# One ScalarE operation for phi of 18 sums, small operations moved to GpSimd, and a new order of all instructions

## The chip, the cores and the metric

The program runs on one core of a Trainium2 chip. The metric is the device time of one execution in microseconds, the median of three runs. A core has five engines with an in-order queue each: TensorE (PE in the profile; its weight loads PEld), VectorE (DVE), ScalarE (ACT), GpSimd (POOL) and SyncE (SP), which here only issues DMAs. They wait for one another by semaphores.

## The reference, cut to what matters

```python
x  = A_x                                   # 2048 tokens x 512, fp32
xn = layernorm(x)
q, k, v = split(xn @ wqkv)                 # 32 heads of 16
phi = lambda t: where(t > 0, t + 1, exp(t)) + 1e-6
kv, z = einsum(phi(k), v), sum(phi(k))     # per head
s  = (phi(q) @ kv / (phi(q) . z + 1e-6)) @ wo
g  = silu((gelu(x @ w_gate) * (x @ w_up)) @ w_down)    # of the same xn; F = 1792
out = x + s * g
```

## The kernel before, in words

Everything is fp32 made from pairs: each operand is split into a high part `h` (rounded) and a low part `l` (the rest), and each product is three TensorE passes, h·h, h·l and l·h. On top of that the large products use a seven-product Strassen scheme (`PRODUCTS`), in three PSUM banks X, Y and Z: product 1 goes into X, ScalarE copies X to Y (the "seed"), product 2 is added to Y and product 6 to X; ScalarE saves X (`u2`), product 7 is added, X is saved again (`u3`), product 4 is added to X, and products 5 and 3 go into Z. VectorE adds a saved tile and Z (`added`, tiles `c22` and `c12`).

The 2048 tokens are 16 tiles of 128, taken as 8 pairs `n`. Per pair, for q and k:

- `ln` normalises: statistics on VectorE (`bn_stats`, `bn_aggr`), the addition of eps to the variance (`ve`, VectorE), a power of -1/2 on GpSimd (`rstd`), and xn on VectorE (first pairs) or ScalarE (`xn`, with bias and scale from tiles).
- xn is turned: the first pairs by TensorE (`pt`), the later ones by a write to DRAM (`xn_d`), a read (`xq`) and VectorE's transpose (`xt`).
- `forms` makes the Strassen sums `T` on GpSimd; `split` makes `Xh` (ScalarE) and `Xl` (VectorE).
- Pairs 0 and 1 take plain products, pairs 2 to 7 the scheme above. Of each pair there are four results: k from Y, q from c22, q from X, k from c12. `phi` turns each into phi by two ScalarE operations, relu(-v) into a tile `r` and exp(-r) in place (L708, L709), and one VectorE operation max(v,0)+r into a tile `p0` (L711; `kp` or `qp` in the trace). `r` has two places and `p0` four, taken in turn, so a new `qp` waits until the DMA of the one four before it (`q_d<-qp`) has landed.
- `split_xn` sets a column of xn to one (L686, VectorE) and splits xn; `gacc` then accumulates xn^T·phi(k) in four PSUM banks (`gps`); the column of ones gives the sum z.

Meanwhile some FFN weights are prepared (`tmp`, `we`, written to `w_d`). From about 125 us on the FFN runs in two halves of 1024 tokens with gate, up and down products (FX, FY, FZ and dX, dY, dZ), and the attention's last product (`sps`) is put between its last passes.

The order of the instructions on every engine is set by one list of numbers, `ORDER`: the code records some 3600 operations with their dependencies, and `plan.order()` emits them as the list says. The list was searched beforehand with a model of durations and of transfer times that were scattered at random.

Of the kernel before, what the change touches and what calls it, by code (L numbers as in the profile page):

```python
# [18 lines left out]
    2, 4, 1, 0, 993, 3, 6, 7, 9, 10, 11, 8, 16, 15, 17, 23, 5, 18, 19, 14, 55, 24, 13, 12, 56, 27, 57, 20, 58, 115, 61, 60, 62, 28, 64, 116, 117, 66,  # L19
    68, 118, 59, 25, 119, 67, 89, 88, 35, 120, 65, 80, 26, 91, 82, 74, 93, 79, 121, 21, 77, 104, 122, 90, 123, 124, 22, 33, 148, 98, 149, 36, 126, 73,  # L20
    71, 69, 38, 76, 72, 151, 102, 95, 34, 63, 132, 78, 75, 96, 37, 108, 81, 150, 105, 94, 313, 140, 127, 83, 134, 141, 315, 99, 31, 287, 138, 100,
    125, 136, 314, 289, 131, 84, 101, 133, 288, 152, 316, 142, 153, 290, 103, 92, 139, 291, 137, 85, 319, 292, 135, 106, 317, 128, 107, 320, 109, 178,
    86, 170, 318, 173, 110, 181, 180, 293, 322, 425, 143, 158, 171, 167, 154, 295, 155, 111, 296, 70, 427, 174, 298, 172, 112, 176, 177, 129, 175,
    299, 426, 163, 297, 161, 230, 294, 29, 232, 428, 234, 401, 226, 300, 113, 233, 301, 321, 30, 179, 302, 229, 87, 164, 231, 144, 399, 307, 160, 224,
    182, 223, 145, 187, 305, 47, 165, 166, 32, 190, 183, 306, 225, 228, 400, 431, 156, 402, 245, 97, 239, 162, 309, 308, 243, 159, 184, 146, 244, 250,
    403, 227, 303, 39, 240, 404, 49, 241, 256, 328, 304, 311, 248, 40, 157, 258, 235, 323, 265, 263, 41, 266, 236, 255, 246, 114, 51, 264, 260, 42,
    262, 261, 208, 237, 257, 45, 259, 247, 405, 188, 249, 43, 429, 276, 407, 282, 267, 242, 46, 238, 281, 202, 185, 197, 196, 251, 279, 44, 273, 278,
    252, 272, 147, 919, 274, 277, 268, 253, 271, 275, 189, 269, 280, 254, 192, 283, 191, 186, 408, 284, 203, 310, 327, 168, 285, 325, 326, 52, 286,
    206, 331, 218, 199, 215, 410, 312, 193, 920, 341, 409, 411, 340, 324, 53, 342, 270, 130, 922, 332, 343, 367, 406, 333, 346, 921, 348, 169, 412,
    349, 923, 347, 511, 413, 350, 200, 54, 334, 415, 414, 198, 207, 335, 219, 417, 513, 194, 222, 336, 358, 512, 419, 514, 440, 210, 329, 337, 356,  # L30
    418, 924, 357, 479, 515, 211, 925, 926, 516, 359, 212, 201, 214, 614, 360, 927, 221, 195, 205, 420, 338, 361, 216, 209, 344, 517, 330, 362, 518,
    384, 438, 616, 439, 520, 519, 615, 217, 48, 437, 928, 521, 430, 204, 443, 386, 522, 213, 50, 220, 421, 930, 375, 444, 368, 422, 446, 423, 929,
    445, 523, 441, 617, 339, 345, 931, 447, 452, 618, 351, 619, 454, 528, 543, 453, 369, 940, 352, 385, 527, 455, 442, 381, 363, 353, 620, 376, 424,
    383, 623, 459, 354, 460, 932, 624, 529, 461, 365, 462, 364, 524, 448, 534, 380, 470, 621, 469, 449, 532, 525, 468, 622, 366, 379, 533, 934, 471,
    377, 416, 378, 355, 382, 526, 472, 456, 535, 631, 458, 450, 473, 457, 370, 933, 489, 540, 371, 463, 542, 935, 536, 541, 582, 625, 451, 477, 626,
    546, 432, 495, 474, 491, 538, 476, 372, 433, 556, 434, 539, 373, 494, 630, 555, 537, 936, 493, 435, 547, 464, 937, 557, 646, 549, 717, 941, 558,
    387, 632, 548, 530, 943, 393, 550, 562, 942, 374, 475, 465, 564, 944, 563, 627, 392, 565, 388, 637, 497, 490, 719, 480, 498, 635, 488, 551, 718,
    492, 720, 571, 466, 628, 636, 395, 573, 478, 572, 721, 552, 394, 722, 560, 481, 574, 487, 638, 391, 496, 818, 575, 561, 482, 397, 723, 576, 389,
    398, 724, 559, 531, 643, 629, 633, 725, 483, 644, 819, 566, 938, 645, 939, 820, 396, 649, 390, 580, 544, 821, 578, 822, 823, 639, 651, 545, 553,
    579, 659, 484, 726, 592, 650, 640, 567, 599, 727, 658, 581, 641, 467, 660, 634, 485, 728, 652, 824, 747, 642, 577, 661, 663, 583, 664, 554, 501,  # L40
    945, 486, 667, 568, 665, 732, 584, 509, 653, 947, 666, 946, 825, 507, 503, 569, 948, 500, 654, 601, 729, 436, 595, 591, 668, 502, 662, 655, 597,
    730, 674, 733, 590, 676, 675, 669, 736, 499, 677, 594, 786, 504, 600, 949, 737, 505, 678, 681, 950, 951, 738, 596, 740, 679, 510, 952, 506, 585,
    508, 685, 826, 593, 731, 739, 647, 744, 961, 745, 586, 746, 656, 587, 682, 750, 683, 648, 953, 702, 741, 759, 734, 955, 753, 588, 954, 751, 827,
    589, 752, 956, 742, 761, 657, 828, 693, 754, 570, 735, 608, 696, 684, 829, 760, 613, 743, 762, 701, 610, 606, 957, 607, 697, 609, 755, 958, 959,
    695, 603, 670, 604, 833, 756, 766, 962, 686, 960, 768, 680, 671, 602, 963, 612, 1200, 765, 672, 964, 699, 767, 830, 688, 764, 769, 611, 965, 763,
    834, 831, 605, 775, 966, 776, 832, 748, 837, 968, 777, 770, 700, 778, 704, 967, 698, 838, 598, 779, 703, 969, 783, 757, 780, 694, 999, 839, 782,
    841, 673, 784, 840, 835, 846, 689, 785, 845, 758, 803, 847, 970, 690, 864, 972, 851, 795, 971, 865, 771, 687, 973, 794, 691, 860, 842, 1094, 787,
    853, 692, 852, 772, 749, 861, 843, 862, 788, 974, 714, 854, 844, 863, 976, 805, 855, 866, 975, 715, 856, 773, 705, 977, 868, 848, 869, 836, 789,
    774, 857, 711, 781, 867, 790, 887, 1050, 716, 870, 800, 791, 710, 713, 1099, 801, 871, 877, 978, 1100, 708, 792, 796, 980, 876, 979, 872, 878,
    793, 981, 884, 1095, 873, 712, 997, 879, 706, 874, 707, 883, 1101, 1096, 808, 1102, 814, 875, 709, 885, 1097, 849, 807, 1138, 886, 817, 880, 812,  # L50
    798, 1201, 858, 804, 797, 799, 1098, 890, 859, 802, 806, 809, 891, 815, 1269, 811, 1105, 881, 904, 901, 1002, 895, 888, 892, 902, 896, 1108, 850,
# [107 lines left out]
    3569, 3560, 3545, 3566, 3568, 3529, 3470, 3617, 3471, 3562, 3561, 3469, 3474, 3475, 3585, 3538, 3463, 3464, 3465, 3575, 3466, 3570, 3573, 3591,  # L159
    3574, 3546, 3616, 3472, 3547, 3578, 3539, 3607, 3530, 3477, 3579, 3479, 3478, 3473, 3610, 3480, 3622, 3580, 3614, 3467, 3584, 3602, 3563, 3615,  # L160
    3586, 3564, 3608, 3571, 3476, 3623, 3606, 3587, 3609, 3619, 3601, 3588, 3600, 3628, 3611, 3572, 3627, 3620, 3599, 3612, 3621, 3624, 3531, 3625,
    3613, 3630, 3626, 3631, 3598, 3633, 3632, 3634, 3603, 3635, 3604, 3605,
]

TABLES = {"exp": "exp", "gelu": "gelu", "silu": "silu"}
# [1283 lines left out]
```

## Time and profile before

| what | value |
|---|---|
| runs | 568.57, 568.45, 567.86 us; median 568.45 |
| the profiled execution's own time | 568.69 us |
| its span, first to last instruction | 567.0 us |
| granted TensorE clock | 1.000 |
| PE busy | 556.9 us (98%), 2620 matmuls |
| DVE, ACT, POOL busy | 491.4 (87%), 358.1 (63%), 216.4 us (38%) |

A PE that is busy 98% of the span may still run slower than it could, since a matmul's end in the profile is modelled: a matmul that reads 512 columns is shown with 379 ns, while matmuls follow one another more closely than that. The distance from one start to the next is what tells of a wait. In the rows of the timeline the columns are: start in us, duration in us, engine, line, operation, written tile <- read tiles, shapes, count, and in brackets the idle time of the engine before it and what ended it. `SPq` is SyncE's queue issuing a DMA. A row with x2 or more is several instructions in a row, from the first start to the last end.

### The profile page before, as it was taken

How to read it: one execution, taken by the hardware profiler on the slowest of the kernel's cores; microseconds unless marked ns; L12 is line 12 of the kernel's file. 1: busy time of each engine (PE TensorE's matmuls, PEld its weight loads, DVE VectorE, ACT ScalarE, POOL GpSimd, SP SyncE). 2: the span in 40 equal slices, each digit the busy share in tenths (PEclk: the TensorE clock that was granted, in tenths of full speed). 3: DMA queues.
4: the chain of work that ended last, by engine and by line, in shares of the span. 5: the costliest groups of instructions: out<-in, count | busy, mean ns of one | idle time of the engine just before them, and what ended most of it. 6: DMA issues, size and time to landing. Idle time of an engine off the chain costs nothing.

```text
span 567.0 us, 7903 instructions
## 1 busy us (share of the span) xinstructions
PE 556.9 (98%) x2620; PEld 485.2 (86%) x2620; DVE 491.4 (87%) x793; ACT 358.1 (63%) x662; POOL 216.4 (38%) x222
## 2 busy tenths in 40 slices
PE   7999999999999999999999999999999999999996
PEld 6888887888988888888888888888888888888885
DVE  6999998797599999999978886956688898998996
ACT  5987888796667775663546267957553635465531
POOL 4724342436767867304045652410214040324000
PEclk9999999999999999999999999999999999999999
DMA  8577989887778865458867898886645567668885
GB/s 282 149 209 238 291 266 269 255 253 232 305 268 322 312 236 202 144 206 286 304 212 287 324 410 319 265 344 221 242 149 205 205 215 281 228 189 267 279 260 210
DMA packets 82362, 143.71 MB, mean 253 GB/s; under 512 B 5393, under 2 KB 50449, under 8 KB 78354
## 3 DMA queue, kind: packets, MB, share of 16 engines
q1 hardware_dynamic: 82322, 143.22, 74.0%
q8 instruction: 20, 0.33, 0.2%
q14 instruction: 20, 0.16, 0.1%
HBM read 89.19 MB, written 54.00 MB: 253 GB/s over the span
## 4 chain that ended last, share of the span: by engine, by line
PE 95%; DMA 2%; DVE 2%; ACT 1%; SPq 0%; issue 0%; DVEq 0%; ACTq 0%
PE FX L443 26%; PE dX L443 13%; PE FZ L443 13%; PE sps L443 7%; PE dY L443 6%; PE gps L443 6%; PE FY L443 6%; PE X L443 5%; PE dZ L443 3%; PE Z L443 3%; PE k L443 2%; PE q L443 2%; PE Y L443 1%; DMA x<-in_A_x 1%; DMA q_d<-qp 1%; PE pkv L978 1%
## 5 line engine op out<-in xcount | busy, mean ns | idle before, releaser
L443 PE MATMUL FX<-Xh,w 128*128 128x512 f32 x448 | 125.7, 379 | 0.0
L443 PEld LDWEIGHTS FX<-Xh,w 128*128 128x128 f32 x448 | 84.5, 189 | 12.0
L405 POOL TENSOR_TENSOR sums<-draw 128x256 f32<-128x256 f32 x28 | 24.6, 882 | 128.3 <-DMA draw<-in_B_w_down 77.3
L399 ACT COPY dY<-dX 128x512 f32<-128x512 f32 x56 | 32.1, 574 | 63.1 <-DVE acc L1109 39.4
L443 PE MATMUL FX<-Xl,w 128*128 128x512 f32 x224 | 66.3, 380 | 0.1
L443 PE MATMUL FZ<-Xh,w 128*128 128x512 f32 x224 | 64.3, 379 | 0.0
L1155 POOL TENSOR_TENSOR h<-h,g 128x512 f32<-128x512 f32 x28 | 39.8, 1422 | 50.6 <-DVE h L405 42.7
L399 ACT COPY fu<-FX 128x512 f32<-128x512 f32 x56 | 32.6, 584 | 33.6 <-PE FX L443 25.4
L405 POOL TENSOR_TENSOR tmp<-raw 128x256 f32<-128x256 f32 x28 | 26.7, 964 | 57.8 <-DVE we L405 22.7
L443 PEld LDWEIGHTS FX<-Xl,w 128*128 128x128 f32 x224 | 42.2, 189 | 6.3 <-PE dX L443 0.4
L443 PEld LDWEIGHTS FZ<-Xh,w 128*128 128x128 f32 x224 | 42.3, 189 | 6.0
L405 DVE TENSOR_TENSOR hfl<-sums,hfh 128x512 fp32r<-128x512 f32 x56 | 44.8, 804 | 2.2 <-ACT hfh L399 2.1
L443 PE MATMUL dX<-hfl,dh 128*128 128x512 f32 x112 | 41.7, 380 | 0.2 <-DVE hfl L405 0.2
L443 PE MATMUL dX<-hfh,dl 128*128 128x512 f32 x112 | 41.8, 380 | 0.0
L443 PE MATMUL dX<-hfh,dh 128*128 128x512 f32 x112 | 41.5, 379 | 0.0
L399 ACT CAST hfh<-sums 128x512 fp32r<-128x512 f32 x56 | 34.3, 620 | 10.2 <-DVE sums L405 8.9
L1109 DVE TENSOR_TENSOR acc<-acc,dY 128x512 f32<-128x512 f32 x48 | 32.6, 680 | 9.2 <-PE dY L443 9.2
L1109 DVE TENSOR_TENSOR acc<-acc,dX 128x512 f32<-128x512 f32 x48 | 32.5, 680 | 6.2 <-PE dX L443 5.8
L405 DVE TENSOR_TENSOR hfl<-h,hfh 128x512 fp32r<-128x512 f32 x42 | 32.6, 781 | 2.1 <-ACT hfh L399 2.0
L443 PE MATMUL FZ<-Xl,w 128*128 128x512 f32 x112 | 33.0, 379 | 0.0
L443 PE MATMUL FY<-Xh,w 128*128 128x512 f32 x112 | 33.0, 379 | 0.0
L946 POOL TENSOR_TENSOR qz<-qz,zq 128x512 f32<-128x512 f32 x16 | 23.1, 1442 | 21.5 <-DMA qz<-q_d 11.9
(217 smaller groups left out, 1473.4 us busy)
## 6 DMA issues: line engine op xcount, KB each, us to landing
w<-w_d SPq DMA_DIRECT2D x17, 1792.0 KB, 7.6
w_d<-w SPq DMA_DIRECT2D x11, 1792.0 KB, 8.4
draw<-in_B_w_down SPq DMA_DIRECT2D x14, 512.0 KB, 4.4
w_d<-we SPq DMA_DIRECT2D x18, 256.0 KB, 2.2
x<-in_A_x SPq DMA_DIRECT2D x16, 256.0 KB, 4.3
q_d<-qp SPq DMA_DIRECT2D x16, 256.0 KB, 3.3
qz<-q_d SPq DMA_DIRECT2D x16, 256.0 KB, 3.2
q<-q_d SPq DMA_DIRECT2D x16, 256.0 KB, 3.8
```

The lines of the kernel that those rows point to most:

```text
L399: do("ACT", act(n, src.psum), lambda o, i: nc.scalar.copy(o, i), dst, src, name=name)
L405: do(eng, c, lambda o, p, q: getattr(e, f"tensor_{op}")(o, p, q), dst, a, b, name=name)
L443: nc.tensor.matmul(o if r is None else o[:, r], a, turned(b), start=first, stop=made == self.passes[r], skip_group_check=self.on or r is n ...
L946: do("POOL", pool(D), lambda o, z: nc.gpsimd.tensor_mul(o, o, z.unsqueeze(1).to_broadcast([P, KT, P])), rows_of(q), zq, name="u")
L978: nc.tensor.matmul(o[:, g, :], ab[c][:, g * P:(g + 1) * P], ab[KT + c][:, g * P:(g + 1) * P], start=(c == 0), stop=(c == KT - 1))
L1109: do("DVE", dve(D), lambda o, i: nc.vector.tensor_add(o, o, i), o, ps, name="acc")
L1155: do("POOL", pool(NC), lambda o, i: nc.gpsimd.tensor_mul(o, o, i), h, g, name="h")
```

## The change

For v that is a sum of two tiles (c22, c12) the addition adds 1 as well, so that the tile holds v+1; for k from Y the seed copies X+1 into Y. phi is then max(v+1, min(exp(v),1)): one ScalarE operation exp with a bias tile of -1, and one VectorE operation. These are three of four results of pairs 2 to 7, 18 in all; the fourth (q from X) and the plain ones stay as they were. The eps addition to the variance and the column of ones go from VectorE to GpSimd. `XA` is an empty list, so its branches do nothing.

```diff
+    neg_one = tile_in("sm", "no", [P, 1], F32, "neg_one")
+    do("DVE", 0.1, lambda o: nc.vector.memset(o, -1.0), neg_one, port=False)
...
-        do("DVE", 0.1, lambda o, i: nc.vector.tensor_scalar_add(o, i, EPS_LN), ve, mv[:, :, 1])
+        do("POOL", 0.1, lambda o, i: nc.gpsimd.tensor_scalar_add(o, i, EPS_LN), ve, mv[:, :, 1])
...
-        do("DVE", 0.1, lambda o: nc.vector.memset(o, 1.0), (x[0] if isinstance(x, tuple) else x)[:, 0:1], name="one", port=False)
+        do("POOL", 0.12, lambda o: nc.gpsimd.memset(o, 1.0), (x[0] if isinstance(x, tuple) else x)[:, 0:1], name="one")
...
     def added(e, ps, name, places=("c", range(19, 22))):
         c = U(*places, name)
-        tt("DVE", "add", c, e, ps, D, name)
+        do("DVE", 0.6, lambda o, i, j: nc.vector.scalar_tensor_tensor(o, i, 1.0, j, op0=ALU.add, op1=ALU.add), c, ps, e, name=name)
...
-    def phi(v, t, nm):
+    def phi(v, t, nm, plus=False):
         r = U("r", range(22, 24), f"{nm}r{t}")
+        if plus or not v.psum:
+            do("ACT", act(D), lambda o, i, b: nc.scalar.activation(o, i, AF.Exp, bias=b), r, v, neg_one, name="exp")
+            p0 = U("p", range(24, 28), f"{nm}p{t}")
+            do("DVE", 0.6, lambda o, i, j: nc.vector.scalar_tensor_tensor(o, i, 1.0, j, op0=ALU.min, op1=ALU.max),
+               p0, r, v, name="phi")
+            return p0
         do("ACT", act(D), lambda o, i: nc.scalar.activation(o, i, AF.Relu, scale=-1.0), r, v, name="relu")
         do("ACT", act(D), lambda o, i: nc.scalar.activation(o, o, AF.Exp, scale=-1.0), r, r, name="exp")
...
-        copy("ACT", Y, X, D, "seed")
+        do("ACT", act(D), lambda o, i: nc.scalar.activation(o, i, AF.Copy, bias=1.0), Y, X, name="seed")
         prod(Y, n, 2, False)
-        k_out(Y, ta)
+        k_out(Y, ta, True)
```

The numbers of `ORDER` are replaced as a whole:

```diff
 ORDER = [
-    2, 4, 1, 0, 993, 3, 6, 7, 9, 10, 11, 8, 16, 15, 17, 23, 5, 18, 19, 14, 55, 24, ...
```

TensorE does the same 2586 matmuls of the program (the profile's 2620 count some of the 128-wide ones twice), in another order. Three places follow. In the names, the number after the last underscore tells one buffer's use from another's; xN in a row is a count.

TensorE at the start, from the first transposes to the first products, before:

```order
L642 MATMUL pt_166<-blk,xn_160 128x128 x4
L471 MATMUL warm<-blk 128x128 x2
L642 MATMUL pt_193<-blk,xn_186 128x128 x4
L443 MATMUL k_205<-kq_141,Xh_177 128x512
L443 MATMUL k_205<-kq_141,Xl_191 128x512
L443 MATMUL k_205<-kq_141,Xh_177 128x512
```

and now:

```order
L655 MATMUL pt_162<-blk,xn_158 128x128 x4
L472 MATMUL warm<-blk 128x128 x2
L442 MATMUL k_181<-kq_138,Xh_175 128x512
L655 MATMUL pt_196<-blk,xn_187 128x128 x4
L442 MATMUL k_181<-kq_138,Xl_192 128x512 x2
L442 MATMUL k_181<-kq_138,Xh_175 128x512 x3
```

The first product stands ahead of the second group of transposes.

TensorE in pair 6, from product 1 in X to the next writing of X (product 6, which waits until ScalarE has read X for the seed), before:

```order
L443 MATMUL X_1204<-kq_141,Xh_177 128x512 x4
L443 MATMUL X_1204<-kq_141,Xl_191 128x512 x2
L443 MATMUL Z_1104<-kq_200,Xh_177 128x512 x2
L443 MATMUL Z_1104<-kq_200,Xl_191 128x512 x2
L443 MATMUL gps_405<-pkh_1214,xnh_1202 128x512
L443 MATMUL X_1204<-kq_175,Xh_177 128x512 x2
```

and now:

```order
L442 MATMUL X_1197<-kq_138,Xl_192 128x512 x2
L442 MATMUL X_1197<-kq_138,Xh_175 128x512 x2
L442 MATMUL Z_1109<-kq_246,Xl_192 128x512 x2
L442 MATMUL gps_381<-pkh_1201,xnh_1193 128x512
L442 MATMUL Z_1109<-kq_246,Xh_175 128x512 x4
L442 MATMUL gps_368<-pkh_994,xnl_1051 128x512
L442 MATMUL gps_347<-pkl_1097,xnh_1036 128x512
L442 MATMUL X_1197<-kq_177,Xh_175 128x512 x2
```

Five matmuls stood between the two, and nine do now.

VectorE at pair 5's phi of c22 (`qp<-c_5`), which needs the landing of an earlier `q_d<-qp`, before:

```order
L711 SCALAR_TENSOR_TENSOR kp_1289<-Y_1220,kr_1255 128x512
L711 SCALAR_TENSOR_TENSOR qp_1310<-c_5_1166,qr_1284 128x512
L616 STREAM_TRANSPOSE xt_1316<-xq_1263 128x4x4x32
L616 STREAM_TRANSPOSE xt_1316<-xq_1287 128x4x4x32
L405 TENSOR_TENSOR Xl_191<-xt_1316,Xh_177 128x4x128
```

and now:

```order
L629 STREAM_TRANSPOSE xt_1292<-xq_1253 128x4x4x32
L629 STREAM_TRANSPOSE xt_1292<-xq_1269 128x4x4x32
L724 SCALAR_TENSOR_TENSOR kp_1317<-kr_1309,Y_1217 128x512
L714 SCALAR_TENSOR_TENSOR c_6_1323<-Z_1265,u_6_1288 128x512
L404 TENSOR_TENSOR Xl_192<-xt_1292,Xh_175 128x4x128
L730 SCALAR_TENSOR_TENSOR qp_1341<-X_1197,qr_1325 128x512
L724 SCALAR_TENSOR_TENSOR qp_1348<-qr_1262,c_5_1190 128x512
```

The phi stood ahead of the pair's two transposes; it now comes behind them and four other operations. On SyncE the write that it waits for (`q_d<-qp_1119`) is issued as the second after the read `xq_1269` that the second transpose waits for.

16 lines of the change are left out of this document (14 added, 2 removed), and 287 rows, old and new, of the table ORDER.

## The prediction

> **What bounds the kernel now.** I read the page's first part, then the busy time by windows, the chain of waits, and the timeline wherever TensorE's starts lie further apart than usual.
>
> ```profile
> span 567.0 us, 7903 instructions
> PE 556.9 (98%) x2620; PEld 485.2 (86%) x2620; DVE 491.4 (87%) x793; ACT 358.1 (63%) x662; POOL 216.4 (38%) x222
> ```
>
> ```profile
> core 0: us, PE busy (x) PEld busy (x) DVE busy (x) ACT busy (x) POOL busy (x), PEclk, DMA share, GB/s
> 38.00:125.00 87.00, 85.93 (x397) 73.36 (x395) 78.94 (x144) 72.12 (x134) 33.46 (x40) 1.00 0.86 260
> 125.00:310.00 185.00, 185.00 (x874) 162.06 (x873) 165.25 (x249) 117.44 (x224) 99.23 (x94) 1.00 0.72 254
> 310.00:480.00 170.00, 169.75 (x785) 147.66 (x784) 135.17 (x204) 99.88 (x182) 48.77 (x47) 1.00 0.74 266
> ```
>
> ```profile
> 13.18 7.34 PE k L443 x34
> ```
>
> ```profile
> L642 PE MATMUL pt<-blk,xn x8: 272/272/273, 37.9 to 45.1; 128*128 128x128 f32 x8
> ```
>
> TensorE is the bound, at a full granted clock (1.00). Its undisturbed pace is the chain's row of 34 matmuls in 7.34 us: 0.216 us each. So the windows tell how much waiting is left. From 38 to 125 us (pairs 2 to 7) 397 matmuls, of which 8 are transposes of about 0.11 us, need 389 x 0.216 + 0.9 = 84.9 of 87.0 us: 2.1 us are lost. From 310 to 480 us 785 x 0.216 = 169.6 of 170.0: 0.4 us, and up to 0.3 more, since matmuls cut by the window's edges are counted whole. From 125 to 310 us nothing is lost (874 x 0.216 is already more than 185; some are narrow). Outside of this stands the start, and an end of 5 us. No edit makes TensorE's own work smaller, so 2.1 + 0.7 us, and what the start gives, is all that can be won; ScalarE's and VectorE's time counts only where it ends one of these waits.
>
> The waits from 38 to 125 us, from the timeline (the write's row is from the chain of waits):
>
> ```profile
> 90.19 1.10 DVE L616 STREAM_TRANSPOSE xt<-xq 128x512 f32<-128x512 f32 x1 [1.49 <-DMA xq<-xn_d]
> 91.14 0.67 DVE L405 TENSOR_TENSOR c<-u,Z 128x512 f32<-128x512 f32 x1
> 91.18 0.38 PE L443 MATMUL gps<-pkh,xnh 128*128 128x512 f32 x1
> 91.86 0.70 PE L443 MATMUL Z<-kq,Xh 128*128 128x512 f32 x2 [0.30 <-DVE xn L686]
> ...
> 95.24 0.59 PE L443 MATMUL Z<-kq,Xl 128*128 128x512 f32 x2
> 95.62 0.57 ACT L399 COPY Y<-X 128x512 f32<-128x512 f32 x1
> 95.77 0.48 PE L443 MATMUL gps<-pkh,xnh 128*128 128x512 f32 x1
> 96.25 0.70 PE L443 MATMUL X<-kq,Xh 128*128 128x512 f32 x2
> ```
>
> ```profile
> 98.74 5.06 DMA q_d<-qp
> ```
>
> ```profile
> 103.89 1.26 DVE L711 SCALAR_TENSOR_TENSOR qp<-c,qr 128x512 f32<-128x512 f32 x1 [1.68 <-DMA q_d<-qp]
> 105.19 0.63 ACT L708 ACTIVATE kr<-c 128x512 f32<-128x512 f32 x1 [2.21 <-DVE qp L711]
> 105.20 0.38 PE L443 MATMUL gps<-pkh,xnh 128*128 128x512 f32 x1
> 106.35 0.92 PE L443 MATMUL X<-kq,Xh 128*128 128x512 f32 x3 [0.77 <-ACT u L399]
> ```
>
> (a) At 91 us VectorE sat 1.49 us at a transpose whose read had not landed; the addition c behind it was late, and product 3 in Z with it: from 91.18 to 91.86 is 0.68, less a pace of 0.22 makes 0.46, and 0.1 for the restart (0.70 for two matmuls instead of 0.59). (b) At 96 us ScalarE reached the seed late; product 6 comes 0.26 us late, with 0.10 just before and 0.10 of restart: 0.46. (c) At 105 us the phi of c22 waited for a write that took 5.06 us; ScalarE's next relu wanted the tile r that this phi holds, and the copy u behind it came late: 1.15 - 0.22 = 0.93, and 0.10. The three make 2.05, so they are the whole loss of this stage.
>
> Later on the largest is
>
> ```profile
> 319.20 1.89 PE L443 MATMUL sps<-Xl,M 128*128 128x512 f32 x8
> 320.00 1.12 DVE L405 TENSOR_TENSOR hfl<-sums,hfh 128x512 fp32r<-128x512 f32 x1
> 321.27 0.46 PE L443 MATMUL dX<-hfl,dh 128*128 128x512 f32 x1 [0.18 <-DVE hfl L405]
> ```
>
> Eight matmuls from 319.20 end their pace at 320.93, so 0.34 us are lost to a VectorE operation that took 1.12 us.
>
> **The change part by part.**
>
> *phi.* Prices:
>
> ```profile
> L709 ACT ACTIVATE qr<-qr 128x512 f32<-128x512 f32 x13 | 8.2, 629 | 0.2
> L564 ACT ACTIVATE xn<-x,nb,rstd 128x512 f32<-128x512 f32 x8 | 6.4, 807 | 0.3 <-DVE nb L560 0.2
> L554 DVE TENSOR_SCALAR ve<-mv 128x2 f32<-128x2 f32 x7 | 1.7, 241 | 0.0
> ```
>
> ```profile
> 0.30 0.10 POOL L1423 MEMSET const-float32-0.0<- 128x1 f32 x1 [0.30 <-issue]
> ```
>
> 18 relus of 0.63 us go, 11.3 us of ScalarE. The exp that stays takes its bias from a tile: no row has just that, the two nearest are 0.63 (numbers in the instruction) and 0.81 (bias and scale both from tiles); I take the middle, 0.72, which takes back 18 x 0.09 = 1.6 us (ends 0 and 3.2). ScalarE is busy 72.1 of 87.0 us in this stage, so some 62.5 remain. On the path it counts where a result hangs on phi: a hand-off is shorter by one operation, about 0.5 us. VectorE's part keeps its count and its kind; the added constant costs nothing beside 512 columns. The seed with +1 is the same copy. The memset of -1 stands at the start, where VectorE waits for x: nothing; ahead of the first statistics it would cost about the 0.10 that GpSimd's memset of a column takes.
>
> *GpSimd.* 16 memsets of a column and nine additions, seven of them 0.24: some 2 us less on VectorE, and the memsets besides. On GpSimd a memset of one column is 0.10; the addition isn't shown there; its bounds are that 0.10 and the 0.82 of the line below, a power of two inputs; I take 0.25, 16 x 0.10 + 9 x 0.25 = 3.9 us on an engine that is busy 33 of 87 us. It lies ahead of a power that stood on GpSimd already, so a crossing between engines goes too. Behind these operations on GpSimd stand the sums T, which ScalarE's Xh waits for; a memset there waits for the read of its xn, but the T behind it needs that same DMA's data, so nothing is added. If the addition cost 0.8, only the start would feel it (below).
>
> ```profile
> L556 POOL TENSOR_TENSOR rstd<-ve,neg_half 128x2 f32<-128x2 f32 (+1 forms) x9 | 7.4, 824 | 12.8 <-DVE ve L554 12.5
> ```
>
> *The order at the start.*
>
> ```profile
> 8.59 0.65 ACT L399 CAST Xh<-pt 128x256 fp32r<-128x256 f32 x2 [1.05 <-PE pt L642]
> 9.21 0.62 ACT L399 CAST kq<-wk 128x512 fp32r<-128x512 f32 x1
> 10.01 0.74 DVE L405 TENSOR_TENSOR Xl<-pt,Xh 128x256 fp32r<-128x256 f32 x2
> 10.07 0.66 PE L642 MATMUL pt<-blk,xn 128*128 128x128 f32 x4 [1.08 <-DVE xn L572]
> 10.49 0.46 PE L443 MATMUL k<-kq,Xh 128*128 128x512 f32 x1
> ```
>
> The first six DMAs stand in the same order, so x comes as before. Now one product goes before the second transposes, at about 8.9, when the first half of Xh is cast. The second half stands behind one more cast kq (9.21 to 9.83) and takes 0.33, so it is done by 10.16, or 0.1 earlier as far as ScalarE's operations overlap. Xl waits for both halves and takes 0.37 a half: 10.4 and 10.8, and with it the second and third product at 10.45 and 10.8 and the fourth at 11.0. Before, the first is at 10.49 and the fourth at 11.14 or, with a restart of 0.1, 11.24: 0.2 us gained. Ends: 0.5 gained if the second half of Xh isn't late, 0.5 lost if a later hand-off of the start misses.
>
> *The order in pairs 2 to 7.* Loss (c): the phi now comes behind two transposes and four operations. The read that the second transpose waits for is issued two places ahead of the phi's write, at most 1 us earlier. From issue to landing the two kinds took
>
> ```profile
> DMA to landing us min/median/max: 3.4/4.2/5.4
> DMA to landing us min/median/max: 2.3/3.3/8.6
> ```
>
> (reads xq, then the writes and reads of q_d). Transpose 1.1 and four operations of 0.6 after 4.2 make 7.7 us from the read's issue, where the write, even with the 5.06 of this case, is landed by 6.1. I let all 1.03 go. Loss (b): there were five matmuls between product 1 and product 6, 1.08 us, for a hand-off of 0.2 (end of a matmul) and 0.65 (seed); nine now give 1.94, and a relu less stands ahead of seeds: all 0.46 goes. Loss (a): an addition c still stands behind transposes, so half of 0.56: 0.28. What comes late next: any other transpose or phi behind a slow DMA. Such waits fell on two places of this stage before; I put 0.35 for new ones, between 0 and 1.6 (both places anew).
>
> *Order after 125 us.* Nothing of the computation changes there. The places with little to spare lie elsewhere: I take back half of the 0.7, 0.35 (ends 0.7 gained, 0.8 lost).
>
> *The end.*
>
> ```profile
> 560.30 0.42 DVE L1323 TENSOR_TENSOR acc<-acc,sps 128x256 f32<-128x256 f32 x1 [0.57 <-PE sps L443]
> 562.00 0.69 DVE L1325 TENSOR_TENSOR acc<-acc,sps 128x512 f32<-128x512 f32 x1
> 562.72 0.69 DVE L405 TENSOR_TENSOR acc<-acc,sxr 128x512 f32<-128x512 f32 x1
> ```
>
> Again a 512-wide tile is last, with one product, one addition and one DMA behind it; the halves are done 8 matmuls (1.73 us) earlier, as long as VectorE's four half operations take (560.30 to 562.00 here): 0, at most 0.4 if they stand one deeper.
>
> Sum: -0.2 - 1.03 - 0.46 - 0.28 + 0.35 - 0.35 = -2.0 us. The profiled execution took 568.69 us, 1.7 us around its span, and 0.24 us above the median of the three runs. 568.69 - 2.0 = 566.7; with the median as start it would be 566.4. I say 566.6.
>
> **The rivals.**
>
> *The waits come back elsewhere.* For it: two of the three losses were DMAs that landed late, and a new order meets other DMAs. Against it: VectorE has 2 us and ScalarE 10 us more room in 87. Only the start is gained: 568.69 - 0.2 = 568.5, no change that can be measured (what a measurement of this kernel can tell is about 0.2%, 1.1 us: below 567.3 is faster, above 569.6 slower).
>
> *GpSimd and VectorE hold each other up.* The 1.12 us of hfl and 1.26 of qp above are long beside the 0.67 of the addition c, which has as many elements. In the start three additions stand in GpSimd's queue; if each is held for a VectorE operation of 0.7, the last xn comes 2.1 late against some 0.7 to spare (an estimate: wanted by TensorE at 12.1, its chain ends near 11.4), so the start loses 1.4 instead of gaining 0.2: 566.7 + 1.6 = 568.3, no change. The Trainium skill (SBUF — State Buffer, section "SBUF: two separate sides") goes that way: VectorE with two SBUF inputs and GpSimd take a shared port pair by an exclusive lock, and the loser is blocked for the whole instruction; by that rule the additions, which read SBUF, would pay this and the time be 568.3, without it 566.7; the trace agrees in the lengthening, and shows no operation held for the whole of another.
>
> *Slower: the phi's writes land late in every pair.* The slowest DMA on q_d took 8.6 us. Behind the read by 1 us it lands at 9.6, against 7.7 covered: VectorE waits 1.9, and of that the 1.1 us that the nine matmuls above leave are to spare, so 0.8 a pair. From four pairs on (3.2) it decides: 566.7 + 3.2 = 569.9. Against it: the median is 3.3, and one wait of 16 was seen.
>
> *The change doesn't shorten ScalarE's chain.* At the upper end, exp 0.81, two operations of 0.63 still become one; excluded.
>
> **How the numbers follow.** Forecast 0.55, by itself 565.9 to 567.3; waits come back 0.24; port 0.08; slower 0.13. Nothing can go below all losses gone with 0.5 at the start: 568.69 - 2.05 - 0.7 - 0.5 = 565.4. To leave out 2 in 10 the range reaches over both rivals without change to the lower part of the slow one: 565.4 to 569.4. Faster: the forecast and a little of the second, 0.57; same 0.30; slower 0.13.
>
> **What the profile of the changed kernel would show.** Right: the window 38 to 125 us with 1 us or less lost against 0.216 us a matmul; no wait of phi for `q_d<-qp`; ScalarE's busy time down by about 10 us; exp with the bias tile near 0.72; the fourth product of the start at about 11.0. Wrong: a start that pauses after the first product beyond 10.6; phi or a transpose waiting over 1.5 us for a DMA twice or more; TensorE waiting after 125 us for more than 0.7 us.

## The result, and the profile after

The changed kernel takes 564.46 us (median of four runs, 564.29 to 565.16) against 568.15 beside it; the ratio is 0.9940, with a 95% interval of 0.9927 to 0.9953. Run twice more it gave 565.17 (0.9957, 0.9943 to 0.9972) and 565.51 us (0.9949, 0.9929 to 0.9968). So it is about 2.9 us faster (2.4 to 3.4 by the three ratios of 568 us), where 2.0 was forecast and 565.4 called the floor.

The page's first lines, then the two windows that lost time before:

```profile
span 562.6 us, 7886 instructions
PE 555.7 (99%) x2620; PEld 486.6 (86%) x2620; DVE 486.0 (86%) x769; ACT 353.5 (63%) x646; POOL 216.7 (39%) x247
```

```profile
38.00:125.00 87.00, 87.00 (x406) 75.89 (x405) 79.28 (x132) 65.73 (x118) 33.55 (x54) 1.00 0.87 266
...
310.00:480.00 170.00, 170.00 (x790) 148.86 (x789) 137.84 (x210) 101.75 (x182) 45.53 (x45) 1.00 0.74 264
```

Nine more matmuls fit into pairs 2 to 7 (406 against 397) and five more into 310 to 480 us (790 against 785). The list of what TensorE waited for says the same; its columns are the total in us, the times, and the longest. Before:

```profile
PE pt L642 <- DVE xn L572: 2.6, 2, 1.5
PE warm L471 <- DVE blk L463: 1.1, 1, 1.1
PE X L443 <- ACT u L399: 0.8, 1, 0.8
PE Z L443 <- DVE xn L686: 0.3, 1, 0.3
PE dX L443 <- DVE hfl L405: 0.2, 1, 0.2
```

and after, where nothing is left behind the first transposes:

```profile
PE pt L655 <- DVE xn L585: 1.3, 2, 0.7
PE warm L472 <- DVE blk L462: 1.1, 1, 1.1
```

The prices foretold, from the groups of instructions after: exp with the bias tile, the eps addition on GpSimd, the column of ones.

```profile
L722 ACT ACTIVATE qr<-c,neg_one 128x512 f32<-128x512 f32 x6 | 4.3, 718 | 0.0
L722 ACT ACTIVATE kr<-Y,neg_one 128x512 f32<-128x512 f32 x6 | 4.1, 689 | 1.0 <-PE Y L442 0.9
L556 POOL TENSOR_SCALAR ve<-mv 128x2 f32<-128x2 f32 x7 | 2.5, 357 | 1.2 <-DVE mv L554 1.2
L699 POOL MEMSET xn<- 128x1 f32 x16 | 1.2, 97 | 4.9 <-DMA xn_d<-xn 4.9
```

To compare kernels stage by stage I sum, over all matmuls, by how much the distance to the next start exceeds the pace (0.216 us for 512 columns, half for 256). The sums hold constants (0.2 to 0.4 us around the transposes up to 125 us, 1.8 from 125 to 310 us), so only their differences tell. Each row is one profiled execution; "x4" is the landing of the fourth x, "last" the time from issue to landing of the last write; the kernels are those of the experiments below.

| kernel | x4, us | 38-125 | 125-310 | 310-480 | last, us | span |
|---|---|---|---|---|---|---|
| before | 8.50 | 2.91 | 1.80 | 0.99 | 2.47 | 567.0 |
| before_again | 7.63 | 1.67 | 1.80 | 1.52 | 3.18 | 566.4 |
| before_third | 7.95 | 2.15 | 1.83 | 0.69 | 3.18 | 566.2 |
| changed | 7.94 | 0.43 | 1.85 | 0 | 2.02 | 562.6 |
| after_again | 8.44 | 0.38 | 1.93 | 0 | 2.01 | 563.2 |
| after_third | 8.51 | 0.56 | 1.85 | 0 | 2.02 | 563.5 |
| old_order_new_vector | 7.77 | 0.89 | 2.94 | 1.15 | 2.01 | 565.1 |
| old_order_new_phi | 8.12 | 1.09 | 1.80 | 1.32 | 2.01 | 564.9 |
| old_order_new_ops | 7.73 | 1.37 | 1.89 | 1.56 | 2.01 | 564.9 |
| new_order_old_ops | 8.14 | 3.81 | 3.02 | 0.76 | 2.02 | 568.4 |
| new_order_old_phi | 8.05 | 3.05 | 3.03 | 0 | 2.01 | 566.5 |
| new_order_old_vector | 8.43 | 1.41 | 1.85 | 0.09 | 2.01 | 564.4 |

Between the first two profiled executions (567.0 to 562.6) the 4.3 us are 2.5 in pairs 2 to 7, 1.0 from 310 to 480 us, 0.45 at the last write, and 0.5 at the start. By the means of three executions of each kernel the spans differ by 3.4 us: 1.8 in pairs 2 to 7, 1.1 from 310 to 480 us and 0.9 at the last write, less 0.3 at the start, where the fourth x landed later in the changed kernel's three.

### The profile page after: what moved, and what is told of

Read it like the earlier page. It is cut to its first block, busy times and chain, and to the rows that moved or that the text cites. A ratio compares the mean times of both kernels' runs of the same rounds, so it can differ in the third digit from the quotient of the medians.

```text
span 562.6 us, 7886 instructions
## 1 busy us (share of the span) xinstructions
PE 555.7 (99%) x2620; PEld 486.6 (86%) x2620; DVE 486.0 (86%) x769; ACT 353.5 (63%) x646; POOL 216.7 (39%) x247
## 4 chain that ended last, share of the span: by engine, by line
PE 98%; DMA 1%; DVE 1%; SPq 0%; issue 0%
PE FX L442 26%; PE FZ L442 13%; PE dX L442 13%; PE sps L442 7%; PE gps L442 7%; PE dY L442 6%; PE FY L442 6%; PE X L442 6%; PE dZ L442 3%; PE Z L442 3%; PE k L442 2%; PE q L442 2%; PE Y L442 1%; DMA x<-in_A_x 1%; PE pkv L997 1%; PE pt L655 1%
## 5 line engine op out<-in xcount | busy, mean ns | idle before, releaser
L442 PE MATMUL FX<-Xh,w 128*128 128x512 f32 x448 | 127.6, 380 | 0.0
L404 DVE TENSOR_TENSOR hfl<-sums,hfh 128x512 fp32r<-128x512 f32 x56 | 42.0, 756 | 1.3 <-ACT hfh L398 1.3
L404 DVE TENSOR_TENSOR hfl<-h,hfh 128x512 fp32r<-128x512 f32 x42 | 30.3, 721 | 0.3 <-ACT hfh L398 0.2
```

Source lines behind the costliest of these rows:

```text
L404: do(eng, c, lambda o, p, q: getattr(e, f"tensor_{op}")(o, p, q), dst, a, b, name=name)
L442: nc.tensor.matmul(o if r is None else o[:, r], a, turned(b), start=first, stop=made == self.passes[r], skip_group_check=self.on or r is n ...
```

## The experiments

### Order and operations apart

My theory was that the new order carries the gain, the rival that the operations do. The old phi in the new order (in new_order_old_ops together with the next edit):

```diff
-            do("ACT", act(D), lambda o, i, b: nc.scalar.activation(o, i, AF.Exp, bias=b), r, v, neg_one, name="exp")
+            def two(o, i):
+                nc.scalar.activation(o, i, AF.Relu, bias=1.0, scale=-1.0)
+                nc.scalar.activation(o, o, AF.Exp, scale=-1.0)
+            do("ACT", act(D), two, r, v, name="exp")
```

The old vector work in the new order:

```diff
-        do("POOL", 0.1, lambda o, i: nc.gpsimd.tensor_scalar_add(o, i, EPS_LN), ve, mv[:, :, 1])
+        do("DVE", 0.1, lambda o, i: nc.vector.tensor_scalar_add(o, i, EPS_LN), ve, mv[:, :, 1])
...
-        do("POOL", 0.12, lambda o: nc.gpsimd.memset(o, 1.0), (x[0] if isinstance(x, tuple) else x)[:, 0:1], name="one")
+        do("DVE", 0.1, lambda o: nc.vector.memset(o, 1.0), (x[0] if isinstance(x, tuple) else x)[:, 0:1], name="one", port=False)
```

The kernels with the old order take the list ORDER of before, each number replaced by that of the same operation in the changed program (`old_order_new_ops`); `old_order_new_phi` has the edit just above besides, and `old_order_new_vector` is the kernel before with that edit the other way round.

> The changed kernel's order with the old operations in it: phi of the 18 sums is again two ScalarE operations (relu(1-(v+1)), then exp of its negative) at the place of the one, and eps additions and ones columns are on VectorE. Theory (the new order carries the gain: its hand-offs have at least 0.37 us to spare where the old order had seven with 0.3 or less): 0.3 to 0.8 us slower than the changed kernel, 564.8 to 565.3 us. Rival (shorter phi and relieved VectorE carry it, the order only moves waits): at least 2.5 us slower, 567 us or more.

> The old order, with each old number mapped to the same operation of the changed program (18 relus left out, the memset of -1 behind that of -1/2), and all new operations. Theory (order): the hand-off at 96 us gains by the missing relu, 0.3 to 0.5 us, the waits for DMAs at 91 and 105 us and the start stay: 567.3 to 568.2 us. Rival (operations): 566 us or less, with the loss from 38 to 125 us down to 0.5 us or less.

> The changed kernel with phi of the 18 sums as two ScalarE operations again (11 us more on ScalarE); eps additions and ones columns stay on GpSimd. Theory (order): 0.2 to 0.6 us slower than the changed kernel, 564.6 to 565.1 us. Rival (the shorter phi carries the gain): 2 us or more slower, 566.5 us or more, with TensorE waiting for products that hang on ScalarE from 38 to 125 us.

> The changed kernel with the 9 eps additions and 16 ones columns on VectorE again, at their places in the order. Theory (order): within 0.3 us of the changed kernel, 564.2 to 564.8 us. Rival (VectorE's relief carries the gain): 1 us or more slower, 565.5 us or more. A third (GpSimd and VectorE hold each other up): faster than the changed kernel by 0.3 us or more.

> The old order with the shorter phi alone; eps additions and ones columns on VectorE. Theory (ScalarE's queue ahead of the hand-offs): the gain of all new operations in the old order, 1.3 us, comes back whole: 566.4 to 567.4 us. Rival (VectorE's relief is half of it): 567.5 us or more.

> The kernel before with the 9 eps additions and 16 ones columns on GpSimd, nothing else changed. Theory (phi carries it): within 0.5 us of the kernel before. Rival (VectorE's relief): 0.6 us or more faster. A third (GpSimd and VectorE hold each other up at their shared port): 0.6 us or more slower.

| ratio to before (95% interval) | old operations | new vector work | new phi | both |
|---|---|---|---|---|
| old order | 1 | 0.9979 (0.9966-0.9992) | 0.9984 (0.9968-1.0000) | 0.9976 (0.9959-0.9992) |
| new order | 1.0021 (1.0012-1.0030) | 1.0002 (0.9992-1.0011) | 0.9953 (0.9941-0.9966) | 0.9940, 0.9957, 0.9949 |

My theory fell. The new order with the old operations takes 569.32 us, 1.2 more than before, the old order with all new ones 566.94, 1.4 less; together they are worth 2.9. In the old order either half of the new operations gives as much as both, within the intervals. Phi is the piece the new order needs: without it (568.42) the gain is gone, and with it, but with VectorE's old work (565.74), nearly all is there.

Where the old phi hurts is seen at once, since both kernels emit the same order. In new_order_old_phi TensorE waited, among others, for

```profile
PE FX L442 <- DVE qp L733: 0.8, 1, 0.8
PE pt L655 <- DVE xn L585: 0.7, 1, 0.7
PE X L442 <- ACT u L398: 0.6, 1, 0.6
PE Z L442 <- DVE c L714: 0.4, 1, 0.4
```

The wait for u, from its timeline (start, duration, engine), and then the same place after the change:

```profile
87.00 0.61 ACT L723 ACTIVATE kr<-c 128x512 f32<-128x512 f32 x1
87.62 0.59 PE L442 MATMUL Z<-kq,Xl 128*128 128x512 f32 x2
87.65 0.63 ACT L724 ACTIVATE kr<-kr 128x512 f32<-128x512 f32 x1
88.19 0.57 ACT L398 COPY u<-X 128x512 f32<-128x512 f32 x1
...
88.81 0.48 PE L442 MATMUL X<-kq,Xh 128*128 128x512 f32 x1 [0.59 <-ACT u L398]
```

```profile
85.14 0.71 ACT L722 ACTIVATE kr<-c,neg_one 128x512 f32<-128x512 f32 x1
85.91 0.59 ACT L398 COPY u<-X 128x512 f32<-128x512 f32 x1
```

TensorE may not write X again until u has copied it. With one operation u ends at 86.5, and X's next product starts at 87.43, in step; with two, u ends at 88.76, and that product 0.76 us later against the other execution, with 0.10 for the restart. Counting from matching matmuls (times of the changed kernel), the 18 relus cost 0.48 at 63 to 65 us, 0.86 here, 0.18 at 92, 0.68 at 106, 0.32 at 109 and 1.10 at 124.5 us, where the first FX needs the bank that the last phi frees: 3.6 of the 3.9 us between the two ends.

### Three relus, and the other fifteen

```diff
+            def exps(o, i, b, old=((nm, t) in (("k", 9), ("k", 12), ("q", 15)))):
+                if old:
+                    nc.scalar.activation(o, i, AF.Relu, bias=1.0, scale=-1.0)
+                    nc.scalar.activation(o, o, AF.Exp, scale=-1.0)
+                else:
+                    nc.scalar.activation(o, i, AF.Exp, bias=b)
```

(`fifteen_relus`: `not in`.)

> The changed kernel with only three of its 18 phi as two ScalarE operations again: k from Y of pair 5 and k from c12 of pair 4, which stand one behind the other ahead of the copy u that product 7 in X waits for, and q from c22 of pair 7, which stands ahead of the phi that frees the bank of the first FX. Theory (a relu costs only where a hand-off hangs on the queue behind it): the two steps that all 18 relus gave at these places, 0.86 and 1.10 us, come back whole: 1.6 to 2.1 us slower than the changed kernel, 566.1 to 566.6 us. Rival (the price goes with ScalarE's work, 3 of 18 of 4.0 us): 0.7 us slower, 565.2 us or less.

> The complement of the three relus: the changed kernel with the other 15 of its 18 phi as two ScalarE operations, those three as one. All 18 together cost 4.0 us, the three alone 0.8. Theory (a backlog: ScalarE is some 0.5 to 1 us behind when it reaches a hand-off, by all the relus ahead of it, and the last operation tips it over): 2.6 us slower than the changed kernel or less, 565.8 to 567.1 us, with the step at 124.5 us under 0.5 us. Rival (each place has its own price): 3.2 us or more slower, 567.7 us or more.

Three relus: 565.23 us, 0.9961 (0.9948 to 0.9973), some 0.7 us behind the changed kernel (mean ratio 0.9949). This is the rival's number: the two steps came back as 0.19 and 0.25 us, not 0.86 and 1.10. Fifteen: 567.11 us, 0.9987 (0.9978 to 0.9996), 2.2 us behind, with 0.25 at 124.5 us. At 124.5 us, then, three relus cost 0.25, the other fifteen 0.25, and all 18 cost 1.10: no single operation owns this wait. It fits a backlog, in which ScalarE comes to a hand-off late by what all earlier relus have left it behind, and the last ones tip it over. By the mean ratios the two add up to 2.9, against 3.0 for all 18.

The places in the profiles don't repeat exactly. The largest part of the three relus' 1.3 us, 0.60, fell at 106 us, and that is not ScalarE's hand-off alone: VectorE waited there for a read of xq, in three_relus and, below, in the changed kernel:

```profile
104.19 1.09 DVE L629 STREAM_TRANSPOSE xt<-xq 128x512 f32<-128x512 f32 x1 [1.31 <-DMA xq<-xn_d]
```

```profile
103.14 1.10 DVE L629 STREAM_TRANSPOSE xt<-xq 128x512 f32<-128x512 f32 x1 [0.39 <-DMA xq<-xn_d]
```

The read was issued 0.6 us later, behind an xn that ScalarE ended 1.0 us later, and it took 5.4 us in place of 4.9. In start_undone (below), which has no relu more, it took 5.5 us, and 0.39 us were lost at the same place. So part of the price at 106 us belongs to the read.

### What belongs to the program before, and what to one execution

> The kernel before, unchanged, in one more profiled execution. Theory (its three losses at 91, 96 and 105 us come from one read of xq that took 5.42 us from issue to landing; in the three other kernels with the old order it took 4.1 to 4.4 and none of the three shows): under 1.2 us lost from 38 to 125 us in place of 2.2, while 1.0 to 1.5 us are lost again from 310 to 480 us, and the last write lands in 2.0 us in place of 2.47. Rival (the losses belong to the program): the same three places, about 2 us.

> The kernel before, unchanged, a third profiled execution. Theory (draws of the transfers): the fourth product 3.4 us behind the third x's landing wherever that falls; from 310 to 480 us 1.0 to 1.5 us lost again; from 38 to 125 us between 0.5 and 2.5 us, at places that hang on transfers. Rival (the program's own waits): as the first execution, 0.47, 0.27 and 0.93 us at 91, 96 and 105 us.

> The changed kernel, unchanged, with more runs and a second profile. Theory (the new order leaves the late transfers room): 564.3 to 564.8 us median with nearly all runs within 1 us of one another, nothing lost after 125 us. Rival (its first four runs were lucky): a spread as wide as that of the kernel before, over 2 us, and a median of 565.2 us or more.

> The changed kernel, unchanged, beside the two kernels with another start. Theory: 564.4 to 565.2 us median, its first products 3.4 us behind the third x's landing, under 0.3 us lost after 38 us. Rival (the second call's 565.2 us is the rule and the first was lucky): 565.2 us or more.

The windows of before_again and before_third from 38 to 125 and 310 to 480 us:

```profile
38.00:125.00 87.00, 86.86 (x400) 74.35 (x399) 79.50 (x145) 73.09 (x136) 34.89 (x41) 1.00 0.87 264
...
310.00:480.00 170.00, 169.23 (x782) 147.20 (x781) 133.45 (x204) 99.23 (x180) 46.25 (x46) 1.00 0.73 264
```

```profile
38.00:125.00 87.00, 86.52 (x398) 73.93 (x397) 79.00 (x144) 72.59 (x135) 34.89 (x41) 1.00 0.86 262
...
310.00:480.00 170.00, 169.81 (x787) 147.98 (x786) 133.82 (x205) 100.05 (x182) 46.87 (x47) 1.00 0.73 266
```

Of the three losses of pairs 2 to 7 (here without the restarts), (b) is there in all three executions, 0.27 us each. (a) is 0.47, 0.22 and 0.39. (c) is 0.93, 0.24 and 0.24: the phi waits for its write in all three (1.68, 1.11 and 1.15 us), and the larger part of the first one's loss comes from a write that landed later. The place of (a) in before_again:

```profile
89.01 1.10 DVE L616 STREAM_TRANSPOSE xt<-xq 128x512 f32<-128x512 f32 x1 [1.24 <-DMA xq<-xn_d]
...
90.24 0.38 PE L443 MATMUL gps<-pkh,xnh 128*128 128x512 f32 x1
...
90.68 0.70 PE L443 MATMUL Z<-kq,Xh 128*128 128x512 f32 x2
```

The theory was that one late read of xq made all three. It holds for (a) alone. Two kernels of the section on the last write, one_more_copy and one_more_memset, are before with one instruction more. Over these five executions the read took 5.42, 5.32, 5.18, 5.16 and 4.77 us, and (a) is 0.47, 0.39, 0.22, 0.21 and 0, while (b) stays at 0.26 to 0.27 and (c) at 0.24 or more. In the three kernels with the old order and new operations the read took 4.06 to 4.38 us, and (a), (b) and (c) are gone but for 0.4 us at 93 us in one. Why the read lands sooner there isn't settled.

From 310 to 480 us the loss is in every profile with the old order and the old or new operations (0.69 to 1.56), and in none of the changed kernel. Its constant place is the operation hfl, in before and before_again beside a sum on GpSimd; in before_again:

```profile
316.83 1.27 POOL L946 TENSOR_TENSOR qz<-qz,zq 128x512 f32<-128x512 f32 x1 [2.43 <-DVE sums L405]
317.44 1.21 DVE L405 TENSOR_TENSOR hfl<-sums,hfh 128x512 fp32r<-128x512 f32 x1 [0.68 <-ACT hfh L399]
...
319.17 0.68 DVE L405 TENSOR_TENSOR hfl<-sums,hfh 128x512 fp32r<-128x512 f32 x1
...
320.00 0.45 PE L443 MATMUL dX<-hfl,dh 128*128 128x512 f32 x1 [0.77 <-DVE hfl L405]
```

VectorE's first hfl takes 1.21 us in place of 0.68, and ends 0.55 us behind qz; so the second, which dX needs, ends at 319.85, where TensorE ran out of work at 319.07. This is the wait that the prediction showed at 321.27. The new order leaves no wait there, but it isn't free of others: start_filled (below) lost 0.76 us at 338 us, where dX waited for a copy dY on ScalarE, as new_order_old_ops did at 342 us.

The changed kernel's 15 runs lie between 564.05 and 566.11 us, the 117 of before between 565.5 and 571.2. The changed kernel is steadier, as expected, but its medians in the two later measurements, 565.17 and 565.51 us, are those of the rival.

### The start

`start_undone` moves the entry of the first product behind the second transposes; `start_filled` moves two more products ahead of them. On TensorE, `start_filled` against the changed kernel:

```
+L442 MATMUL k_181<-kq_138,Xh_175 128x512 x3
+L655 MATMUL pt_198<-blk,xn_188 128x128 x4
+L442 MATMUL k_181<-kq_138,Xl_193 128x512 x2
 L442 MATMUL k_181<-kq_138,Xh_175 128x512
-L655 MATMUL pt_196<-blk,xn_187 128x128 x4
-L442 MATMUL k_181<-kq_138,Xl_192 128x512 x2
-L442 MATMUL k_181<-kq_138,Xh_175 128x512 x3
```

On VectorE, `start_dense` against the changed kernel (`start_dense_xn` has the two added operations ahead of both statistics):

```
 L553 BN_STATS st_169<-x_128 128x6
-L553 BN_STATS st_179<-x_130 128x6
-L554 BN_AGGR mv_183<-st_169 128x2
-L554 BN_AGGR mv_183<-st_179 128x2
-L585 TENSOR_SCALAR xn_187<-x_124,mv_155,rstd_167 128x4x4x32
-L404 TENSOR_TENSOR Xl_192<-pt_162,Xh_175 128x2x128 x2
+L585 TENSOR_SCALAR xn_181<-x_124,mv_155,rstd_167 128x4x4x32
+L404 TENSOR_TENSOR Xl_185<-pt_162,Xh_175 128x2x128
+L553 BN_STATS st_187<-x_130 128x6
+L554 BN_AGGR mv_189<-st_169 128x2
+L554 BN_AGGR mv_189<-st_187 128x2
+L404 TENSOR_TENSOR Xl_185<-pt_162,Xh_175 128x2x128
```

> The changed kernel with one entry of its order moved: the first matmuls of the first product stand behind the second transposes again, as before. Theory (the first product ahead gains what the trace shows between the two starts): 0.2 to 0.5 us slower than the changed kernel, 564.7 to 565.0 us. Rival (the earlier landing of x in that execution did it, chance): within 0.2 us.

> The changed kernel with two entries of its order moved: two more matmuls of the first product (they need only the first half of Xh, and weights that are there by 9.3 us) stand ahead of the second transposes, in TensorE's gap from 8.5 to 9.4 us. Theory (TensorE is short of ready work only until 10.0 us; what it does before is won at the end): 0.2 to 0.45 us faster than the changed kernel, 564.0 to 564.3 us. Rival (the second transposes come 0.1 us later and the next transposes wait for xn, so the start is bound by VectorE): no change within 0.15 us, or slower.

> The changed kernel with its start in another order: VectorE's xn of the second x and the first half of Xl stand ahead of the statistics of the fourth x, ScalarE's second half of Xh ahead of a cast that waits for weights, and TensorE takes ten products that need only the first two x ahead of the others. Theory (the start hangs on the third x only through VectorE's queue): the tenth product at about 11.0 us in place of 12.5, and 0.7 to 1.2 us faster than the changed kernel in the same call, 563.6 to 564.3 us. Rival (TensorE waits for the transposes of the next x instead, which hang on the same landings): within 0.3 us of the changed kernel.

> As start_dense, but xn of the second x and the first half of Xl stand ahead of the statistics of the third x too. Theory: the first products no longer follow the third x at all, but the statistics of the third and fourth end 0.5 us later and with them the next transposes: 0 to 0.5 us slower than start_dense, still 0.3 us or more faster than the changed kernel. Rival (nothing hangs on the third x): as start_dense within 0.1 us.

| kernel | median, us | ratio (95% interval) | x4 | product 4 | product 10 | product 30 |
|---|---|---|---|---|---|---|
| before | 568.15 | 1 | 8.50 | 11.22 | 13.45 | 17.77 |
| changed | 564.46 | 0.9940 | 7.94 | 10.73 | 12.47 | 17.23 |
| after_third | 565.51 | 0.9949 (0.9929-0.9968) | 8.51 | 11.29 | 13.03 | 17.78 |
| start_undone | 565.45 | 0.9958 (0.9941-0.9974) | 8.58 | 11.42 | 13.15 | 17.91 |
| start_filled | 565.46 | 0.9955 (0.9939-0.9970) | 7.97 | 10.58 | 12.68 | 17.56 |
| start_dense | 566.27 | 0.9969 (0.9957-0.9982) | 8.06 | 9.78 | 11.16 | 18.16 |
| start_dense_xn | 566.12 | 0.9975 (0.9961-0.9990) | 8.15 | 9.80 | 11.76 | 18.78 |

All four theories failed, start_undone's by its trace alone. start_filled is 0.3 us behind the mean ratio of the changed kernel (0.9949), as its rival said. start_dense is 0.8 us slower than after_third, which ran beside it, where its rival allowed 0.3, and start_dense_xn is no faster. start_undone lies 0.5 us behind the mean ratio with an interval of 0.9 to either side, so its time fits theory and rival alike. The start follows the fourth x (I had named the third; in after_third the fourth product comes 4.30 us behind the third x, 3.4 in the first changed execution, and in both 2.8 behind the fourth): VectorE does its statistics ahead of the xn that the second transposes need. Its rows in before, in the changed kernel, and in after_third (the second of the two statistics in the x2 row starts at 8.05):

```profile
8.71 0.66 DVE L551 BATCH_NORM_STATS2 st<-x 128x6 f32<-128x512 f32 x1
```

```profile
7.35 1.39 DVE L553 BATCH_NORM_STATS2 st<-x 128x6 f32<-128x512 f32 x2 [0.26 <-DMA x<-in_A_x]
...
9.44 0.66 PE L655 MATMUL pt<-blk,xn 128*128 128x128 f32 x4 [0.69 <-DVE xn L585]
```

```profile
8.61 0.69 DVE L553 BATCH_NORM_STATS2 st<-x 128x6 f32<-128x512 f32 x1 [0.91 <-DMA x<-in_A_x]
...
10.01 0.66 PE L655 MATMUL pt<-blk,xn 128*128 128x128 f32 x4 [0.84 <-DVE xn L585]
```

The transposes come 1.36, 1.39 and 1.40 us behind the fourth statistics, whatever stands between. The thirtieth product comes 9.27 to 9.37 us behind the landing of the fourth x in the three executions of before, the three of the changed kernel, and with the start undone: the new order of the start gains nothing, and x4 alone moves it. start_dense does take the first products off that chain (the tenth at 11.16), but then waits for the next transposes, later products come late, and the thirtieth is 0.8 us later:

```profile
11.97 1.00 DVE L585 TENSOR_SCALAR xn<-x,mv,rstd 128x512 f32<-128x512 f32 x2 [0.61 <-POOL xn L699]
...
12.58 0.66 PE L655 MATMUL pt<-blk,xn 128*128 128x128 f32 x4 [0.17 <-DVE xn L585]
13.63 0.70 PE L442 MATMUL k<-kq,Xh 128*128 128x512 f32 x2 [0.40 <-DVE kq L404]
```

None of these beats the changed kernel.

### The last write

What SyncE waits for at the very end, in before, before_third and the changed kernel:

```profile
SPq L1445 <- DMA out_yT<-acc: 2.1, 1, 2.1
```

```profile
SPq L1445 <- DMA out_yT<-acc: 2.8, 1, 2.8
```

```profile
SPq L1464 <- DMA out_yT<-acc: 1.6, 1, 1.6
```

No edit touches this write, and all kernels with another edit had 2.01 or 2.02 us from issue to landing. Two kernels are before with one instruction more:

```diff
+        nc.vector.memset(neg_one(), -1.0)
         nc.vector.memset(o, -0.5)
```

```diff
+            if n == 2:
+                nc.scalar.activation(o[:, 0:1], i[:, 0:1], AF.Copy)
             nc.scalar.copy(o, i)
```

> The kernel before with one instruction more at its start, a memset of a column that nothing reads, on VectorE. Theory (the late landing of the last write belongs to the program before as it stands, not to an operation that the change replaces): the last write lands in 2.0 us, and the kernel is 0.5 to 1.2 us faster than before, 566.6 to 567.4 us. Rival (the three late landings were draws): the same as before within 0.4 us.

> The kernel before with one instruction more on ScalarE, a copy of one column ahead of pair 2's seed that writes what the seed writes anyway (about 0.2 us once). Theory: as one_more_memset, 0.3 to 1.2 us faster than before with a last landing of 2.0 us. Rival (draws): within 0.4 us of before; a third (it hangs on VectorE's instructions alone): 2.5 to 3.2 us for the last landing here, 2.0 us with the memset.

The last write took 2.02 us with the memset on VectorE and 3.18 with the copy on ScalarE: the third reading. In the four executions with a late landing (three of before, and the copy) a load of instructions falls into the write, 1.8 us behind its issue. With the memset it falls 0.1 us behind the issue, and in the other fifteen none falls between the issue and the landing. The row of before_third from 563.8 to 564.0 us (packets, MB, share of the DMA engines' time):

```profile
q14 instruction: 1, 0.01, 9.7%
```

The Trainium skill (Runtime: NRT & Kernel Launch, section "Instruction fetch mechanics") says that each engine's instructions come in blocks by a DMA queue of the engine's own; the trace has two queues of that kind, not one for each of five engines, and one instruction more on VectorE moves the last load, as a block's edge would. That the load delays the write was seen to coincide, not tried. The medians don't show it: 567.72 (0.9995, 0.9978 to 1.0012) and 568.09 (1.0008, 0.9995 to 1.0022). So how much of the 2.9 us is this write stays open between 0 and 1.2.

## Why the prediction was right or wrong, step by step

- **Direction: right, and the reasons half right.** VectorE and ScalarE hand over earlier, the waits of pairs 2 to 7 go, and hardly any new ones come. But the sum credits all its terms to the order, but for one relu less in (b), and has none for the operations: that step failed. In the old order (a), (b) and (c) are gone with either half of the new operations, for (a) because the read landed sooner; and the new order without the shorter phi and the lighter VectorE was slower than before (+1.2 us, against −1.4 for the operations alone and −2.9 for both). The two depend on each other: the new order leaves ScalarE room for one operation, not for two.
- **(c), −1.03, and (b), −0.46: both went in full**; VectorE's list of waits after the change has no phi that waits for `q_d`. But 0.69 of (c) was one execution's: in the others it was 0.24.
- **(a), halved to −0.28: it went whole, 0.57.** In the other two executions of before it was 0.33 and 0.49, behind the same read.
- **The three as the whole loss of the stage, 2.05: too little, 2.5.** Some 0.5 us more lay in steps of 0.04 to 0.17 us at 62 to 64, 78 and 94 us, which a count of matmuls in a window doesn't show. They went too.
- **New waits, +0.35: too many.** Some 0.2 came, at 107 us. Two transposes still waited for their reads (0.66 and 0.39 us at 101.6 and 103.1 us), which cost TensorE nothing.
- **After 125 us, −0.35: too small, −1.0** (0.7 to 1.5 by the other executions of before). Two steps failed: a window with matmuls cut at its edges showed 0.4 us lost where the starts give 0.99, and half of it was kept back though the wait, a tight hand-off to one VectorE operation, belonged to the old order and was in all its profiles.
- **The start, −0.2: the two executions differ by 0.5, the order by nothing.** The landing of the fourth x did it. I took the DMAs as landing where they did before because they were issued in the same order; x4 ranged from 7.63 to 8.51 us in six executions of these two kernels.
- **The end, 0: −0.45**, the last write.
- **The floor of 565.4, and with it the range,** failed by these: it summed TensorE's losses as one execution's windows showed them, and took what lies outside them, the transfers at start and end, as fixed. Between the first two profiled executions 4.3 us went in place of 2.0: 0.3 more in (a), 0.5 in the small steps, 0.15 fewer new waits, 0.65 more after 125 us, 0.3 at the start (luck) and 0.45 at the end.
- **Prices.** exp 0.69 to 0.72 for 0.72: right. The Trainium skill (ScalarE: Activation LUTs, section "What ACT_TABLE_LOAD costs") gives 280 ns and 0.833 ns an element, 0.71 us for 512; the trace agrees. The addition on GpSimd took 0.36 (0.21 to 0.62) for 0.25, the memset 0.10. ScalarE's busy time fell by 8.8 us against the same order with the old phi (362.3 to 353.5), for some 10; against before it fell by 4.6 alone. Of the difference, 2.6 us are two more loads of ScalarE's function tables in the new order, four for three at each of two lines, 1.28 us each; the rest wasn't followed up.
- **The rivals.** The port: the hold is there, its price was wrong. I had read only that some rows are longer. Their ends say more: in before 49 and in the changed kernel 48 of VectorE's 128x512 operations with two input tiles last over 0.8 us in place of 0.68, and every one of them ends 0.54 to 0.56 us behind the end of an operation on GpSimd, as if held until that one was done. GpSimd's additions are held too: 0.23 us alone at 4.53 us, 0.43 at 6.75 us beside VectorE's xn, ending 0.08 behind it. So two holds of 0.2 us fell on the start, not three of 0.7, and the start lost nothing behind x4; in either order moving this work to GpSimd made no median slower beyond the intervals. The phi of (c), 1.10 to 1.26 us long in before's three executions, and the hfl of 1.21 us were such holds. The other two rivals: the waits didn't come back elsewhere, and phi's writes didn't land late in every pair.

## What to carry to other kernels

Where a searched order and shorter operations come together, don't sum their gains: run each alone, since an order tuned to the new lengths can be worse than the old one with the old lengths (here +1.2 alone, −1.4 alone, −2.9 together). Read hand-off losses from several executions of the kernel before, because a single profile mixes the program's own waits, which repeat, with those of one transfer that came late. And when a stage seems to start on the first data, look for what stands ahead in the queue of the engine that feeds it: here the fourth x set the start of work that needs only the first two. When an operation lasts longer than its like, compare its end with the ends on the other engines: a constant distance tells what held it.

## What the hardware showed that I had not expected

The landing of a write with nothing to do with any edit moved from 2.0 to 3.2 us with one instruction on another engine, as above. And in one execution a late start went with a lower clock: in the profiled one_more_memset the fourth x landed at 9.21 us, TensorE stood idle from about 8.0 to 10.75 us, and the granted clock fell to 0.56 from 11 to 14 us and 0.81 from 14 to 16 us; its matmuls were 0.43 us apart in place of 0.216. In the nineteen other profiles TensorE's longest idle stretch between the warm-up matmuls and 16 us was 1.55 us or less, and the clock stayed at 1.00 there.

```profile
11.00:14.00 3.00, 3.00 (x12) 2.35 (x11) 3.00 (x7) 2.36 (x6) 0.62 (x1) 0.56 0.67 219
14.00:16.00 2.00, 2.00 (x13) 1.85 (x12) 2.00 (x6) 1.20 (x3) 0.00 (x0) 0.81 0.60 228
```

Its tenth product came 2.3 us later than in the first execution of before, of which x4's landing explains 0.7. The Trainium skill (TensorE: Matmul & The Clock Gate, section "What's actually happening") puts the array at half rate after an idle window of about 3.4 us; the trace agrees with the half rate, at an idle time of 2.75 us. The new order has one product in that gap; whether it keeps the clock up wasn't tried.
